# One kernel, a new order of its work: the turn of A alternates by head pair, early chunks take whole squares, and PSUM banks are named per product

## The chip, the cores and the metric

The kernel runs on one NeuronCore of a Trainium2 chip. A core has five engines that run side by side, each its own queue of instructions in order: TensorE (PE, matrix products; the loading of its weights is shown as PEld), VectorE (DVE), ScalarE (ACT), GpSimd (POOL) and SyncE (SP), which here only issues transfers. SBUF is the on-chip memory with 128 partitions, PSUM the accumulator memory with eight banks. Engines wait for each other by semaphores.

The metric is the device time of one execution in microseconds. It is compared between the kernel before and the changed one on the same chip.

## The reference

Linear attention with a decay for each head channel, then a feed-forward layer with an unusual activation on every token.

```python
# attention: 4 batches, 8 heads, 768 tokens, head size 48
state = 0
for t in range(768):
    cur = (u * k_t) outer v_t
    y_t = r_t @ (state + cur)
    state = w * state + k_t outer v_t        # w: 0.85 to 0.95 for each head and channel
x = y as [3072 tokens, 384]
# feed-forward, 384 -> 2048 -> 384
h = x @ w_in
g = h * erf(softplus(h))
out = g @ w_out
```

## The kernel before, in words

**Attention.** The 768 tokens are cut into 6 stretches of 128, times 4 batches: 24 chunks `g`, four of each stretch. The recurrence becomes products for each chunk. `K` and `R` scale k and r by powers of the decay (lines 187, 191), `V` (chunks 0 to 3) and `N` make the natural layout of k (201, 208, 195), `Qa`, `Qb`, `Qc` make the diagonal term q = sum of r·u·k (212, 215, 219). `M` lays q on the diagonal of a square for four heads at a time (230, 232). `A` multiplies k and r for each head into a square of 128 by 128 tokens in PSUM (249), `P` copies the half of it that is earlier in time over the `M` square, with a mask (255, copy_predicated). `Y` multiplies v with these squares and with the carried state (272), `D` is the chunk's contribution to the state (291) and `S` updates the state (303 to 309). `X` splits y into a rounded upper part and a rest, the input of the feed-forward layer (312, 315).

**The turn.** Heads come in four pairs; the head `hh` of a pair is 0 or 1. The second head of each pair has its tokens rolled by 64 in k, v and the natural layouts, so that the two heads of a pair fill opposite halves of the systolic array at the same time. `A` skips the quarter of each square that the mask would drop: one half of its products has 64 columns in place of 128, and `P` takes two instructions for a head set, one of 64 by 256 and one of 128 by 256.

**Feed-forward.** Tokens are taken 512 at a time, six blocks `b`, and the 2048 hidden channels 128 at a time: 96 steps of block by hidden slice, twice. Step `f` is nine products into one PSUM bank `h` (338), steps `a b z c d e g h l` make the activation on ACT and DVE (345 to 381; the last one, `l`, on DVE or POOL), and step `p` is nine products of the result into three accumulators (397). `O` moves accumulators out. The weights come as raw 64-bit words and are turned by steps `Ca` to `Cf` into two rounded parts (118 to 130); `F` fetches them.

**What sets the order.** All engines follow one long list of words, ORDER, written out by hand at line 614. Word by word, the kernel emits the step's instructions into the queues; a `+` puts the step on POOL, a `*` on ACT, and no mark on DVE. Within an engine nothing overtakes. `L` issues the two loads of a chunk (66, 69) into the queue of SP, which also runs in order, and a load waits there until its buffer is free: the chunks have three buffers and chunk 3 one of its own. `W` puts products of zeros on PE (87, dummy). PSUM: three banks `h` are handed out in turn to `f`, and before the feed-forward starts to some of the early products; `A0`, `A1` are for attention, `acc0` to `acc2` for the accumulators.

In the opening some 30 attention words and W words run on PE before the first `f` step, f0, which needs the x of chunks 0 to 3 and the first group of weights.

Of the kernel before, what the change touches and what calls it, by code (L numbers as in the profile page):

```python
# [26 lines left out]
P = 128  # L27
C = 128
D = 48
# [11 lines left out]
def body(ctx: ExitStack, tc: tile.TileContext, att, wcol, u, win, wout, levels, outT):  # L41
# [92 lines left out]
    ident = const.tile([P, 2, P], F32, name="ident")  # L134
    mask = const.tile([P, 2, P], F32, name="mask")
# [3 lines left out]
    for o, op, fill in ((ident, ALU.not_equal, 1.0), (mask, ALU.is_gt, 0.0)):  # L139
        for r, hh, j0 in ((slice(0, P), 0, 0), (slice(0, H), 1, H), (slice(H, P), 1, 0)):  # L140
            nc.gpsimd.affine_select(out=o[r, hh], in_=o[r, hh], pattern=[[1, P]], compare_op=op, fill=fill,
                                    base=-j0, channel_multiplier=-1)

# [20 lines left out]
    for r, h0 in ((slice(0, H), 0), (slice(H, PR), H)):  # L164
        nc.scalar.copy(out=wk[r, :, h0:h0 + H], in_=pw[r, 1])
        nc.vector.tensor_tensor(out=wk[r, :, H - h0:C - h0], in0=pw[r, 1],
                                in1=wp[r, 6, 1, :, None].to_broadcast([r.stop - r.start, NPAIR, H]), op=ALU.mult)
# [30 lines left out]
    def turn_k(g):  # L198
        tp = (ps3 if g < 4 else ps1).tile([P, NPAIR, PR], F32, tag="h" if g < 4 else "A1", name=f"kt{g}")
# [23 lines left out]
    def diag_m(q, g, hh, eng):  # L223
# [4 lines left out]
        if eng is nc.scalar:  # L228
            for p in range(NPAIR):
                nc.scalar.mul(out=m[:, p, :], in_=ident[:, hh], mul=q[:, p, hh:hh + 1])  # L230
        else:
            eng.tensor_tensor(out=m, in0=ident[:, hh:hh + 1].to_broadcast([P, NPAIR, C]),
                              in1=q[:, :, hh:hh + 1].to_broadcast([P, NPAIR, C]), op=ALU.mult)
        return m

    def a_step(g):

        t = chunks[g]
        if g in (0, 2):
            ap = [ps3.tile([P, NPAIR, C], F32, tag="h", name=f"A{g}_{hh}") for hh in range(2)]  # L240
        else:
            ap = [ps1.tile([P, NPAIR, C], F32, tag=f"A{hh}", name=f"A{g}_{hh}") for hh in range(2)]
# [10 lines left out]
    def predicated(am, ap, m, hh):  # L253
        for r, c in ((slice(H * hh, H * hh + H), slice(0, H)), (slice(0, P), slice(H, C))):
            nc.vector.copy_predicated(out=am[r, :, c], data=ap[r, :, c],  # L255
                                      mask=m[r, hh:hh + 1, c].to_broadcast([r.stop - r.start, NPAIR, H]))

    def y_step(g):
        s = st_[g]
        s["y"] = y_product(chunks[g], [s["am", 0], s["am", 1]], g % 4, g < 4, f"y{g}", f"acc{g % 2}" if g < 4 else "A0")  # L260

    def y_product(t, am, b, first, name, tag="A0"):
# [4 lines left out]
        y = ps1.tile([P, NQ, C], F32, tag=tag, name=name)  # L267
# [19 lines left out]
    def ds_product(t, first, name):  # L287
        ds = (ps3 if first else ps1).tile([PR, NPAIR, D], F32, tag="h" if first else "A1", name=name)
# [156 lines left out]
    for i, x in enumerate(words):  # L445
        eng = {"+": nc.gpsimd, "*": nc.scalar}.get(x[-1], nc.vector)
# [33 lines left out]
        elif what == "A":  # L480
            st_.setdefault(num, {})
            a_step(num)
        elif what == "P":
            predicated(st_[num // 10]["am", num % 10], st_[num // 10]["ap"][num % 10], mask.bitcast(U32), num % 10)
        elif what == "Y":
            y_step(num)
# [255 lines left out]
```

## Time and profile before

| | us |
|---|---|
| median of 3 runs | 528.97 (525.49 to 532.92) |
| span of the profiled execution | 527.4 |
| PE busy in it | 509.2 |
| ACT busy | 398.6 |
| DVE busy | 350.9 |
| POOL busy | 158.7 |

The span runs from the first to the last instruction. A busy PE is not PE at its peak: matmul records overlap, so 9 products whose records are 0.40 us each end 2.09 us apart as a group. The page cuts the span into 40 slices of 13.2 us. An idle time has a releaser behind it, the instruction whose end let the waiting one go.

### The profile page before, as it was taken

How to read it: one execution, taken by the hardware profiler on the slowest of the kernel's cores; microseconds unless marked ns; L12 is line 12 of the kernel's file. 1: busy time of each engine (PE TensorE's matmuls, PEld its weight loads, DVE VectorE, ACT ScalarE, POOL GpSimd, SP SyncE). 2: the span in 40 equal slices, each digit the busy share in tenths (PEclk: the TensorE clock that was granted, in tenths of full speed). 3: DMA queues.
4: the chain of work that ended last, by engine and by line, in shares of the span. 5: the costliest groups of instructions: out<-in, count | busy, mean ns of one | idle time of the engine just before them, and what ended most of it. 6: DMA issues, size and time to landing. Idle time of an engine off the chain costs nothing.

```text
span 527.4 us, 10451 instructions
## 1 busy us (share of the span) xinstructions
PE 509.2 (97%) x4164; PEld 393.0 (75%) x4164; DVE 350.9 (67%) x610; ACT 398.6 (76%) x765; POOL 158.7 (30%) x147
## 2 busy tenths in 40 slices
PE   7989999899999999999999999999999999999995
PEld 4547777678787778778787787787878777888883
DVE  6999998979787674869587643653664484343442
ACT  4587987889999784877766397767887676786883
POOL 5331225420222440353334434139600230100100
PEclk9999999999999999999999999999999999999999
DMA  8853373332421600531303322040030000010001
GB/s 299 315 195 122 121 251 132 112 128 87 155 99 40 236 21 1 188 155 41 137 1 98 139 88 87 2 162 15 35 115 0 2 1 1 16 45 2 0 1 66
DMA packets 13863, 48.91 MB, mean 93 GB/s; under 512 B 1648, under 2 KB 1776, under 8 KB 13808
## 3 DMA queue, kind: packets, MB, share of 16 engines
q1 hardware_dynamic: 13808, 48.18, 25.9%
q8 instruction: 35, 0.57, 0.4%
q14 instruction: 20, 0.16, 0.1%
HBM read 41.88 MB, written 6.29 MB: 91 GB/s over the span
## 4 chain that ended last, share of the span: by engine, by line
PE 79%; DVE 9%; DMA 4%; ACT 3%; POOL 2%; issue 2%; SPq 1%; POOLq 0%; ACTq 0%
PE h L338 34%; PE acc L397 33%; PE y L272 6%; DMA att<-in_att_dram 4%; PE A L249 3%; PE ds L291 1%; DVE s L370 1%; DVE am L255 1%; DVE wt L125 1%; DVE gl L381 1%; POOL gl L381 1%; PE dummy L87 1%; DVE s L354 1%; DVE wt L120 1%; DVE att L191 1%
## 5 line engine op out<-in xcount | busy, mean ns | idle before, releaser
L338 PE MATMUL h<-x,wih 128*128 128x512 f32 x576 | 183.0, 399 | 1.1 <-DVE s L370 1.1
L338 PEld LDWEIGHTS h<-x,wih 128*128 128x128 f32 x576 | 106.6, 188 | 28.5 <-DVE s L370 2.2
L397 PE MATMUL acc<-gh,woh 128*128 128x512 f32 x288 | 116.5, 404 | 1.4 <-ACT woh L128 1.4
L381 POOL TENSOR_TENSOR gl<-s,gh 128x512 fp32r<-128x512 f32 x43 | 56.7, 1321 | 201.0 <-ACT gh L376 200.9
L397 PE MATMUL acc<-gh,wol 128*128 128x512 f32 x288 | 114.0, 396 | 0.8 <-POOL wol L130 0.6
L397 PE MATMUL acc<-gl,woh 128*128 128x512 f32 x288 | 113.8, 395 | 0.2 <-DVE gl L381 0.2
L338 PE MATMUL h<-x,wil 128*128 128x512 f32 x288 | 113.8, 395 | 0.0
L370 DVE SCALAR_TENSOR_TENSOR s<-s,h 128x512 f32<-128x512 f32 x96 | 65.2, 683 | 63.2 <-ACT s L366 62.9
L354 DVE SCALAR_TENSOR_TENSOR s<-s,h 128x512 f32<-128x512 f32 x96 | 65.5, 684 | 53.1 <-ACT s L349 35.4
L376 ACT CAST gh<-s 128x512 fp32r<-128x512 f32 x96 | 59.1, 616 | 34.5 <-DVE s L370 20.7
L358 ACT ACTIVATE s<-s 128x512 f32<-128x512 f32 x96 | 60.2, 629 | 28.7 <-DVE s L354 28.3
L345 ACT ACTIVATE s<-h 128x512 f32<-128x512 f32 x96 | 56.5, 590 | 27.2 <-PE h L338 27.0
L397 PEld LDWEIGHTS acc<-gh,woh 128*128 128x128 f32 x288 | 54.2, 188 | 17.2 <-issue 2.6
L397 PEld LDWEIGHTS acc<-gh,wol 128*128 128x128 f32 x288 | 54.2, 188 | 14.2 <-POOL wol L130 1.0
L338 PEld LDWEIGHTS h<-x,wil 128*128 128x128 f32 x288 | 54.2, 188 | 12.8
L397 PEld LDWEIGHTS acc<-gl,woh 128*128 128x128 f32 x288 | 54.2, 188 | 12.6 <-DVE gl L381 0.8
L349 ACT ACTIVATE s<-s 128x512 f32<-128x512 f32 x96 | 60.0, 626 | 0.9
L362 ACT ACTIVATE s<-s 128x512 f32<-128x512 f32 x96 | 59.8, 627 | 1.0
L366 ACT ACTIVATE s<-s 128x512 f32<-128x512 f32 x96 | 59.7, 626 | 0.8
L381 DVE TENSOR_TENSOR gl<-s,gh 128x512 fp32r<-128x512 f32 x53 | 40.6, 768 | 19.1 <-ACT gh L376 18.8
L255 DVE COPY_PREDICATED am<-mask,A 64x256 f32<-64x256 uint32 x96 | 39.5, 442 | 11.9 <-ACT am L230 4.0
L230 ACT ACTIVATE am<-ident,q 128x128 f32<-128x128 f32 x100 | 30.8, 389 | 3.1 <-DVE q L219 3.0
(76 smaller groups left out, 498.2 us busy)
## 6 DMA issues: line engine op xcount, KB each, us to landing
att<-in_att_dram SPq DMA_DIRECT2D x24, 608.0 KB, 5.4
att<-in_att_dram SPq DMA_DIRECT2D x24, 512.0 KB, 4.0
raw<-in_win_dram SPq DMA_DIRECT2D x8, 768.0 KB, 4.3
raw<-in_wout_dram SPq DMA_DIRECT2D x8, 768.0 KB, 4.3
out_dram<-o SPq DMA_DIRECT2D x18, 256.0 KB, 2.2
part<-o SPq DMA_DIRECT2D x6, 256.0 KB, 2.1
o<-part SPq DMA_DIRECT2D x6, 256.0 KB, 3.8
ub<-in_u_dram SPq DMA_DIRECT2D x1, 192.0 KB, 2.5
```

What stands on the lines that cost most here:

```text
L255: nc.vector.copy_predicated(out=am[r, :, c], data=ap[r, :, c], mask=m[r, hh:hh + 1, c].to_broadcast([r.stop - r.start, NPAIR, H]))
L338: nc.tensor.matmul(out=h, lhsT=w[:, f, q, :], rhs=x[:, xi, q, :], start=k == 0, stop=k == 8)
L345: nc.scalar.activation(out=s1, in_=e["h"], func=AF.Tanh, bias=FB0, scale=FA0)
L349: nc.scalar.activation(out=s1, in_=s1, func=AF.Tanh, bias=FB1, scale=FA1)
L354: nc.vector.scalar_tensor_tensor(out=e["s"], in0=e["s1"], scalar=FG, in1=e["h"], op0=ALU.mult, op1=ALU.add)
L358: nc.scalar.activation(out=s, in_=s, func=AF.Tanh, bias=FB2, scale=FA2)
L362: nc.scalar.activation(out=s, in_=s, func=AF.Square, bias=FB3, scale=FA3)
L366: nc.scalar.activation(out=s, in_=s, func=AF.Square, bias=FB4, scale=FA4)
L370: nc.vector.scalar_tensor_tensor(out=s, in0=s, scalar=FC, in1=ff[n]["h"], op0=ALU.subtract, op1=ALU.mult, reverse0=True)
L376: nc.scalar.copy(out=e["gh"], in_=e["s"])
L381: eng.tensor_tensor(out=e["gl"], in0=e["s"], in1=e["gh"].bitcast(F32), op=ALU.subtract)
L397: nc.tensor.matmul(out=acc[e], lhsT=w[:, f, es], rhs=g, start=first and i == 0, stop=last and i == 2)
```

## The change

1. **The turn alternates by head pair.** The head that is rolled by 64 tokens is the second one in pairs 0 and 2 and the first one in pairs 1 and 3. `ident` and `mask` get a third square, so that pairs of squares can be read as (0, 1) or (1, 2). The set-up of wk takes four half-size copies and four half-size multiplications in place of two and two.
2. **Whole squares for chunks 0 to 7** (`FULL = 8`): all products of `A` have 128 columns, and `P` is one instruction of 128 by 512 for a head set. For chunks 8 to 23 `P` becomes three instructions: one of 128 by 256 and two of 64 by 128.
3. **Banks named per product**: a word may carry `@` and bank letters (`A0@hh`, `Y10@1`, `D11@0`), so that `A`, `Y` and `D` can lie in `A0`, `A1` or a bank of the ring `h`.
4. **ORDER is a new list** of as many words (1,723). Other words carry `+` and `*`: POOL has 12 more tensor_tensor instructions in all (145 for 133). The zeros of `W` are 62 products in both, 12 of them behind f0 (8 before).

```diff
-    for r, h0 in ((slice(0, H), 0), (slice(H, PR), H)):
-        nc.scalar.copy(out=wk[r, :, h0:h0 + H], in_=pw[r, 1])
+    for r, hh in ((slice(0, H), 0), (slice(H, PR), 1)):
+        for b in range(2):
+            h0 = H * ((hh + b) % 2)
+            nc.scalar.copy(out=wk[r, b::2, h0:h0 + H], in_=pw[r, 1, b::2])
...
-                    jc = abs(c0 - H * hh)
-                    nc.tensor.matmul(out=ap[hh][jc:jc + H, p, i0:C], lhsT=t[r, 512 + p * C + jc:512 + p * C + jc + H],
-                                     rhs=t[r, p * C + i0:(p + 1) * C], start=True, stop=True)
+                    jc = abs(c0 - H * ((hh + p) % 2))
+                    i = 0 if g < FULL else i0
+                    nc.tensor.matmul(out=ap[hh][jc:jc + H, p, i:C], lhsT=t[r, 512 + p * C + jc:512 + p * C + jc + H],
+                                     rhs=t[r, p * C + i:(p + 1) * C], start=True, stop=True)
...
+    def predicated(g, am, ap, m, hh):
+        if g < FULL:
+            nc.vector.copy_predicated(out=by_pair(am), data=by_pair(ap), mask=turned(m, hh))
+            return
+        for r, ps, t, c in ((slice(0, P), slice(0, NPAIR), None, slice(H, C)),
+                            (slice(0, H), slice(hh, NPAIR, 2), 0, slice(0, H)),
+                            (slice(H, P), slice(1 - hh, NPAIR, 2), 1, slice(0, H))):
...
+WARM, FULL = 16, 8
+BANKS = {"0": "A0", "1": "A1", "h": "h"}
...
-U0 L0a L0b L1a K0 T0 L1b R0 V0 Q0a A0 Q0b+ F00 R1+ Q0c N0* M00* W2 D0 S0b K1+ L2a S0a M01* P00 W5 A1 Q1a L2b P01 Q1b+
+U0 L0a L0b W2 K0 Q0a Q0b T0 L1a R1 V0 Q0c M01* L2a M00* L2b N0* R2 R0 L1b K2 F00 Q2a W5 W6 K1 Q1a Q1b+ A0@hh P00 P01
```

Line numbers move: 191, 215, 249, 255, 291, 315, 338, 397 of before are 201, 225, 259, 265, 310, 334, 357, 416 of the changed kernel.

The queue of DVE at the opening, from the first scaling of chunk 0 (its buffer is att_164 before and att_170 in the change; att_167 is chunk 1). Before:

```order
L187 TENSOR_TENSOR att_164<-att_164,wk 112x512
L191 TENSOR_TENSOR att_164<-att_164,wr 112x512
L212 TENSOR_TENSOR att_164<-att_164,ub 128x384
L219 TENSOR_REDUCE q_207<-att_164 128x8
L303 TENSOR_TENSOR sbd<-ds_219,wp 48x4x48 x2
L255 COPY_PREDICATED am_0_211<-mask,A_0_185 64x4x64
L255 COPY_PREDICATED am_0_211<-mask,A_0_185 128x4x64
L212 TENSOR_TENSOR att_167<-att_167,ub 128x384
L255 COPY_PREDICATED am_1_233<-mask,A_1_186 64x4x64
L255 COPY_PREDICATED am_1_233<-mask,A_1_186 128x4x64
```

and in the change (att_186 is chunk 1, att_201 chunk 2):

```order
L197 TENSOR_TENSOR att_170<-att_170,wk 112x512
L222 TENSOR_TENSOR att_170<-att_170,ub 128x384
L225 TENSOR_TENSOR att_170<-att_170 128x384
L201 TENSOR_TENSOR att_186<-att_186,wr 112x512
L229 TENSOR_REDUCE q_194<-att_170 128x8
L201 TENSOR_TENSOR att_201<-att_201,wr 112x512
L201 TENSOR_TENSOR att_170<-att_170,wr 112x512
L197 TENSOR_TENSOR att_201<-att_201,wk 112x512
L222 TENSOR_TENSOR att_201<-att_201,ub 128x384
L197 TENSOR_TENSOR att_186<-att_186,wk 112x512
L222 TENSOR_TENSOR att_186<-att_186,ub 128x384
L265 COPY_PREDICATED am_0_203<-mask,A_0_234 128x512
```

The second product for q0 (line 215, 225 in the change) moved from POOL to DVE, and scalings of chunks 1 and 2 stand where the queue went to the state and the masks of chunk 0.

The queue of SP just behind the loads of chunk 0, before:

```order
L66 DMA att_167<-in_att_dram 128x1024
L69 DMA att_167<-in_att_dram 128x1216
L102 DMA raw_204<-in_win_dram 128x768
L66 DMA att_230<-in_att_dram 128x1024
L69 DMA att_230<-in_att_dram 128x1216
L102 DMA raw_303<-in_wout_dram 128x768
L66 DMA att_328<-in_att_dram 128x1024
L69 DMA att_328<-in_att_dram 128x1216
L66 DMA att_384<-in_att_dram 128x1024
```

and in the change (att_337 is chunk 3, att_388 chunk 4):

```order
L66 DMA att_186<-in_att_dram 128x1024
L66 DMA att_201<-in_att_dram 128x1024
L69 DMA att_201<-in_att_dram 128x1216
L69 DMA att_186<-in_att_dram 128x1216
L102 DMA raw_215<-in_win_dram 128x768
L102 DMA raw_315<-in_wout_dram 128x768
L66 DMA att_337<-in_att_dram 128x1024
L66 DMA att_388<-in_att_dram 128x1024
L69 DMA att_337<-in_att_dram 128x1216
```

Chunk 2 moved ahead of the first weights, and the second half of chunk 3 behind the first half of chunk 4, which waits until a chunk's buffer is free.

On PE, the products D5 and D4 around the third `p` step (p2), before:

```order
L291 MATMUL ds_977<-att_454 48x48 x8
L397 MATMUL acc_0_916<-gh_951,woh 128x512
L397 MATMUL acc_0_916<-gl_956,woh 128x512
L397 MATMUL acc_0_916<-gh_951,wol 128x512
L397 MATMUL acc_1_917<-gh_951,woh 128x512
L397 MATMUL acc_1_917<-gl_956,woh 128x512
L397 MATMUL acc_1_917<-gh_951,wol 128x512
L397 MATMUL acc_2_918<-gh_951,woh 128x512
L397 MATMUL acc_2_918<-gl_956,woh 128x512
L397 MATMUL acc_2_918<-gh_951,wol 128x512
L291 MATMUL ds_1011<-att_384 48x48 x8
L338 MATMUL h_1024<-x_486,wih 128x512 x2
```

and in the change, between p1 and f5:

```order
L416 MATMUL acc_2_909<-gl_903,woh 128x512
L416 MATMUL acc_2_909<-gh_872,wol 128x512
L310 MATMUL ds_928<-att_388 48x48 x8
L310 MATMUL ds_937<-att_472 48x48 x8
L357 MATMUL h_953<-x_383,wih 128x512 x2
```

Two attention products that stood on either side of a feed-forward step stand together. Over the whole list PE goes from an attention product back to `f` or `p` 45 times behind f0 before, and 35 times in the change.

## Rows read from the trace of the kernel before

**Rows 1.** The page: the span, busy time of each engine, and DVE's busy share in 40 slices.

```profile
span 527.4 us, 10451 instructions
PE 509.2 (97%) x4164; PEld 393.0 (75%) x4164; DVE 350.9 (67%) x610; ACT 398.6 (76%) x765; POOL 158.7 (30%) x147
...
DVE  6999998979787674869587643653664484343442
```

**Rows 2.** Windows: busy time of PE, PEld, DVE, ACT and POOL in three stretches (start:end, length, then the engines with their instructions, the clock, DMA).

```profile
7.20:41.30 34.10, 29.86 (x479) 18.21 (x480) 31.74 (x63) 22.44 (x67) 13.93 (x12) 1.00 0.74 277
42.50:123.00 80.50, 76.90 (x682) 58.39 (x679) 73.43 (x116) 68.30 (x128) 25.68 (x21) 1.00 0.39 132
123.00:522.00 399.00, 396.41 (x2958) 313.44 (x2956) 240.06 (x405) 304.53 (x567) 115.27 (x100) 1.00 0.19 66
```

**Rows 3.** Timeline around f0: DVE's last x product of the opening, the end of Y4 on PE, and f0's first products.

```profile
40.77 0.54 DVE L315 TENSOR_TENSOR x<-y,x 128x384 fp32r<-128x384 f32 x1
...
41.52 1.06 PE L272 MATMUL y<-am,att 128*32 128x128 f32 x32
42.51 0.73 PE L338 MATMUL h<-x,wih 128*128 128x512 f32 x2
```

**Rows 4.** Waits of DVE between 7.2 and 41.3 us: total, times, longest.

```profile
DVE q L219 <- POOL att L215: 1.3, 2, 1.1
DVE sbd L303 <- PE ds L291: 0.7, 1, 0.7
```

**Rows 5.** Groups of DVE by form: count, busy us, mean ns, idle before.

```profile
L354 DVE SCALAR_TENSOR_TENSOR s<-s,h 128x512 f32<-128x512 f32 x96 | 65.5, 684 | 53.1 <-ACT s L349 35.4 <-POOL gl L381 16.5
...
L255 DVE COPY_PREDICATED am<-mask,A 64x256 f32<-64x256 uint32 x48 | 21.4, 445 | 11.6 <-ACT am L230 4.0 <-PE A L249 3.8 <-ACT gh L376 1.7
L255 DVE COPY_PREDICATED am<-mask,A 128x256 f32<-128x256 uint32 x48 | 21.1, 439 | 0.3
...
L130 DVE TENSOR_TENSOR wol<-wt,woh 128x768 fp32r<-128x768 f32 x6 | 5.7, 952 | 1.4 <-ACT woh L128 1.4
...
L303 DVE TENSOR_TENSOR sbd<-ds,wp 48x192 f32<-48x192 f32 x8 | 2.8, 353 | 0.7 <-PE ds L291 0.7
```

**Rows 6.** Timeline in the opening: POOL and DVE instructions on SBUF data that ran at the same time.

```profile
28.79 1.00 POOL L215 TENSOR_TENSOR att<-att 128x384 f32<-128x384 f32 x1
28.94 1.40 DVE L191 TENSOR_TENSOR att<-att,wr 112x512 f32<-112x512 f32 x1
...
48.86 0.68 DVE L191 TENSOR_TENSOR att<-att,wr 112x512 f32<-112x512 f32 x1
```

**Rows 7.** Timeline around 215 us: the same on a smaller tile, and it again a little later with POOL idle.

```profile
215.08 1.29 POOL L381 TENSOR_TENSOR gl<-s,gh 128x512 fp32r<-128x512 f32 x1 [20.91 <-ACT gh L376]
215.10 1.48 DVE L309 TENSOR_TENSOR sbd<-sbd,wp 48x192 f32<-48x192 f32 x1
217.46 0.34 DVE L309 TENSOR_TENSOR sbd<-sbd,wp 48x192 f32<-48x192 f32 x1
```

**Rows 8.** The chain that ended last, in order of time (start, us, what): feed-forward steps next to each other, and behind attention products.

```profile
164.87 4.21 PE acc L397 x18
169.07 1.67 PE y L272 x56
170.74 4.40 PE h L338 x18
175.14 0.49 PE ds L291 x16
175.63 2.30 PE h L338 x9
...
184.23 1.02 PE A L249 x24
185.25 4.39 PE acc L397 x18
```

**Rows 9.** Waits of PE, the longest from 42.5 to 123 us (first four) and from 123 us on (last two): total, times, longest.

```profile
PE acc L397 <- ACT woh L128: 1.4, 1, 1.4
PE ds L291 <- DVE am L255: 0.7, 1, 0.7
PE acc L397 <- POOL wol L130: 0.6, 1, 0.6
PE y L272 <- DVE am L255: 0.5, 2, 0.3
...
PE h L338 <- DVE s L370: 0.9, 1, 0.9
PE y L272 <- DVE am L255: 0.8, 1, 0.8
```

**Rows 10.** Timeline of the opening: a wait for a chunk's second half on POOL, and the first load that waits for a free buffer, on SP.

```profile
15.29 1.54 POOL L212 TENSOR_TENSOR att<-att,ub 128x384 f32<-128x384 f32 x1 [0.97 <-DMA att<-in_att_dram]
15.48 0.33 SPq L66 DMA_DIRECT2D att<-in_att_dram  x1
```

**Rows 11.** The end of the chain, the last copy of an accumulator, and PE's dummies before f0.

```profile
519.14 2.14 PE acc L397 x8
...
521.76 0.37 ACT L418 COPY o<-acc 128x256 f32<-128x256 f32 x1 [0.32 <-DVE o L417]
...
39.89 1.02 PE L87 MATMUL dummy<-warm 128*128 128x512 bf16 x4 [0.78 <-PE A L249]
```

More of the change, by code (lines that the diff above doesn't have):

```diff
@@ L198, in turn_k @@
     def turn_k(g):
-        tp = (ps3 if g < 4 else ps1).tile([P, NPAIR, PR], F32, tag="h" if g < 4 else "A1", name=f"kt{g}")
+        tp = bank("h" if g < 4 else "A1", [P, NPAIR, PR], f"kt{g}")
         for p in range(NPAIR):
@@ L229, in diag_m, with bank, a_step @@
             for p in range(NPAIR):
-                nc.scalar.mul(out=m[:, p, :], in_=ident[:, hh], mul=q[:, p, hh:hh + 1])
+                nc.scalar.mul(out=m[:, p, :], in_=ident[:, (hh + p) % 2], mul=q[:, p, hh:hh + 1])
         else:
-            eng.tensor_tensor(out=m, in0=ident[:, hh:hh + 1].to_broadcast([P, NPAIR, C]),
-                              in1=q[:, :, hh:hh + 1].to_broadcast([P, NPAIR, C]), op=ALU.mult)
-        return m
-    def a_step(g):
+            eng.tensor_tensor(out=by_pair(m), in0=turned(ident, hh),
+                              in1=by_pair(q[:, :, hh:hh + 1]).to_broadcast([P, NPAIR // 2, 2, C]), op=ALU.mult)
+        return m
+    def bank(tag, shape, name):
+        return (ps3 if tag == "h" else ps1).tile(shape, F32, tag=tag, name=name)
+    def a_step(g, tags):
         t = chunks[g]
[L239 to L242, printed above, removed]
+        ap = [bank(tags[hh], [P, NPAIR, C], f"A{g}_{hh}") for hh in range(2)]
         for p in range(NPAIR):
@@ L285, in y_product, with ds_product @@
         return y
-    def ds_product(t, first, name):
-        ds = (ps3 if first else ps1).tile([PR, NPAIR, D], F32, tag="h" if first else "A1", name=name)
+    def ds_product(t, tag, name):
+        ds = bank(tag, [PR, NPAIR, D], name)
         for h in range(8):
@@ L445, in body @@
     for i, x in enumerate(words):
+        x, _, where = x.partition("@")
         eng = {"+": nc.gpsimd, "*": nc.scalar}.get(x[-1], nc.vector)
@@ L481, in body @@
             st_.setdefault(num, {})
-            a_step(num)
+            a_step(num, [BANKS[c] for c in where or "01"])
         elif what == "P":
-            predicated(st_[num // 10]["am", num % 10], st_[num // 10]["ap"][num % 10], mask.bitcast(U32), num % 10)
+            predicated(num // 10, st_[num // 10]["am", num % 10], st_[num // 10]["ap"][num % 10], mask.bitcast(U32), num % 10)
         elif what == "Y":
-            y_step(num)
+            y_step(num, BANKS[where] if where else f"acc{num % 2}" if num < 4 else "A0")
         elif what == "X":
@@ L489, in body @@
         elif what == "D":
-            st_.setdefault(num, {})["ds"] = ds_product(chunks[num], num < 4, f"ds{num}")
+            st_.setdefault(num, {})["ds"] = ds_product(chunks[num], BANKS[where] if where else "h" if num < 4 else "A1", f"ds{num}")
         elif what == "S":
@@ new lines @@
+g45 h45 l45 Q17a+ Q17b+ Q17c S12c+ R17+ a47 b47 h46 S11d+ Y15 X15a X15b z47 Y16@1 X16a M171+ M170 A17@0h P170 c47 d47
+D15@h p45 l46 e47 X16b g47 h47 N16+ S15a l47 S13d L18a K18 P171 p46 p47 Y17@1 R18 L18b Q18a+ O311c O471a S15b O470a
+O470b X17a N17 Q18b N18 A18@0h f48 a48 f49 Q18c O471b M181 P181 b48 O472a f50 z48 c48 a49 b49 d48 M180+ P180 X17b e48
+a50 b50 g48 S14d+ Y18 z49 D18 c49 d49 S18a h48 S18b f51 l48 D16 p48 e49 S15c z50 a51 c50 g49 h49 l49+ X18a X18b b51
+z51 d50 e50 f52 L19a K19+ c51 S18c d51 g50 p49 f53 h50 S16a e51 g51 h51 l50+ p50 a52 l51 b52 p51 z52 a53 b53 S16b z53
@@ L702, in turn @@
         x = x.copy()
-        if rows:
-            x.reshape(B * nc_, P, NPAIR, C)[:, 64:] = np.roll(x.reshape(B * nc_, P, NPAIR, C)[:, 64:], C // 2, axis=3)
-        else:
-            x.reshape(B * nc_, C, H, Dh)[:, :, 1::2] = np.roll(x.reshape(B * nc_, C, H, Dh)[:, :, 1::2], C // 2, axis=1)
+        for h in range(H):
+            if (h // 2 + h) % 2:
+                if rows:
+                    s = x.reshape(B * nc_, 2, P // 2, NPAIR, C)[:, h % 2, :, h // 2]
+                    s[:] = np.roll(s, C // 2, axis=2)
+                else:
+                    s = x.reshape(B * nc_, C, H, Dh)[:, :, h]
+                    s[:] = np.roll(s, C // 2, axis=1)
         return x
```

170 lines of the change are left out of this document (87 added, 83 removed).

## Prediction

> **What bounds the kernel now.** I read the page first: PE is busy for 509 of 527.4 us, and DVE's slices are full at the start and fall to a half at the end [rows 1]. Then three windows [rows 2]. From 7.2 to 41.3 us, the opening, DVE works 31.7 of 34.1 us while PE fills its time with dummies. From 42.5 to 123 us PE is idle for 3.6 us of 80.5, with DVE at 73.4 and ACT at 68.3 us close behind it. From 123 to 522 us PE is idle for 2.6 us of 399, and 0.7 us of that lies behind its last product, which ends at 521.3 [rows 11]; DVE has 159 us free there. So there are two stages with different limits: before f0 the queue of DVE, behind f0 the sum of PE's work. f0 itself started at 42.5, when Y4 ended on PE; its last x product had ended 1.2 us sooner, at 41.3 [rows 3]. Last the waits: in the opening DVE waits 1.3 us for POOL and 0.7 for PE [rows 4]; behind f0 PE's waits are single ones of 0.3 to 1.4 us, for weights, masks and an `h` bank [rows 9]. Behind f0 nothing that PE computes goes away, so the change can give: an earlier f0, fewer waits, fewer crossings between attention and feed-forward.
>
> **The sum is made against the profiled span of 527.4 us.** The median of the three runs is 528.97, 1.6 us above it; I add 1.6 at the end.
>
> **1. The opening, f0 earlier by 4.1 us.** Between chunk 0's first scaling and the last x that f0 needs, the two lists give DVE the same 9 scalings of 512 columns, 6 products of 384, 6 reductions and 4 x products. Different are three things. *Masks*: 11 head sets as 22 half instructions, now 10 as whole ones. A half takes 0.44 us alone [rows 5], and follows the one ahead after about 0.40, so 8.8 us. No row shows a mask copy of 512 columns. Its floor is one half, 0.44, its ceiling two, 0.80; I take 0.65, from the nearest row, 512 columns read from PSUM in 0.68 [rows 5], so 6.5 us: 2.3 less (bounds 0.8 and 4.4). *Weights*: the last step of the first w_out group went to POOL: 0.95 less. *State*: one `S` of 0.35 more. DVE's work falls by 2.9 us. Its own waits were 2.4 us of this stretch [rows 2, 4]. The reduction of q0 followed a product on POOL, which is now on DVE, and scalings of chunks 1 and 2 stand where DVE waited for D0. They need their loads, and chunk 2 now comes ahead of the first weights; before, POOL waited 0.97 us for chunk 2's second half, which came at 15.3 behind them [rows 10]. I take half of the idle time back, 1.0 us (bounds 0 and 2.0). The 1.2 us between last x and f0 go too: in the new list four DVE words, about 2 us, stand between the last mask of chunk 4 and the last x, so Y4's 1.67 us run beside them. Against this stand 0.2 us for the set-up of wk (two more small instructions on DVE and on ACT), and 0.8 us for one more meeting of DVE and POOL on SBUF: the row of one such meeting is 1.40 us in place of 0.68 [rows 6]. The third squares of `ident` and `mask` lie on POOL before it has chunk work: nothing. Sum: 2.9 + 1.0 + 1.2 - 0.2 - 0.8 = 4.1 us, f0 at 38.4.
>
> **2. Whole squares on PE: nothing.** `A` for one chunk takes 1.02 us with half its products at 64 columns [rows 8]: 32 records, 32 ns each. `Y` has 56 records, all of 128 columns, in 1.67 us, 30 ns each. So columns up to 128 seem to be free where products of small tiles follow each other. If they are not, `A` costs 256/192 of 1.02, 0.34 us more; of the eight chunks only 6 and 7 lie behind f0, so 0.7 us is the upper bound. The Trainium skill, "TensorEngine Tiling (Array Packing)", section Instruction Overhead, says that a matmul has some 60 cycles of overhead, and that one column takes as long as sixty. By that the 64-column products are just past the overhead, and the whole squares would cost the 0.7 us; the rows of Y speak for nothing, and no run here has shown either.
>
> **3. Fewer crossings: 1.9 us less.** A feed-forward step behind another takes 2.10 us; behind `Y`, `D` or `A` it takes 2.29 or, as a pair, 4.40 in place of 4.21 [rows 8]. That is 0.19 us for each return, 45 before and 35 in the change: 1.9 us. The pair D4, D5 shows one. This rests on PE having no wait there, or else the time goes into the wait (bound 0).
>
> **4. Dummies: 0.85 us more.** Four more zeros stand behind f0, four in 1.02 us with overlap [rows 11], 0.21 each. They cost nothing if PE would wait there.
>
> **5. Waits from f0 to the twelfth `p`: 1.8 us less.** The 3.6 us [rows 2] come from weights and masks that DVE and POOL finish late [rows 9]. By the counts of the two lists DVE has about 5 us less to do between f0 and p12 (masks of chunks 5 to 9, products moved to POOL), PE 1 us less, ACT 3 us less. I take half (bounds: 0, 3.6).
>
> **6. Waits behind that: 1.1 us more.** For chunks 8 to 23 each mask is three instructions. 0.44 for the one of 256 columns, and for 64 by 128 between 0.23 and 0.35 (48 by 192 took 0.35 [rows 5]): 0 to 0.26 us more for each of 32, up to 8 us, beside DVE's 159 free us; uncovered it is 0.26 ahead of a `Y`. What worries more: in the new list several multiplications of the state on POOL, 0.95 us each, stand right ahead of the `Y` that reads the state (S6c and Y10, S11d and Y15, S14d and Y18, S15d and Y19); before, 20 us of PE work lay between. One late word costs up to 1 us, and PE already pays 1.9 us of waits there. I take 1.1 us more, four such places at a quarter of a us (bounds -1.9 and +4). The end of the list keeps its shape: f95, five `p` steps, then 6.1 us of copies and transfer.
>
> **Sum:** 527.4 - 4.1 - 1.9 + 0.85 - 1.8 + 1.1 = 521.55, with 1.6 us: **523.2 us**, 1.1% less.
>
> **Rivals.**
> *All of it fits (chance 0.17).* f0 at 37.5, that is 5.0 us, with every load in time and no meeting with POOL; all 5.5 us of PE's waits gone; crossings 1.9, dummies paid. 527.4 - 5.0 - 5.5 - 1.9 + 0.85 = 515.9, or 517.5 as a run. For it speaks that DVE, the bound of the opening and close to PE behind it, loses work in both. Against it: waits of a list this tight do not all vanish.
> *POOL holds DVE up (chance 0.18), slower than before.* A state product took 1.48 us beside a POOL product that began 0.02 us ahead of it, and 0.34 with POOL idle [rows 7]; the scaling in the opening took 1.40 beside POOL's 1.00 [rows 6]. 12 more POOL instructions, many in the opening and in the stretch to p12 where DVE is the bound, at 0.7 to 1.1 us each, cost DVE 8 to 13 us. Taking 10.5 us with all of it passed on to PE: 521.55 - 0.8 (in term 1 already) + 10.5 = 531.2, 532.8 as a run. It decides the sign from 6.7 us lost on the path, the 5.9 saved and that 0.8. Against it: most meetings fall where DVE has time to spare.
> The Trainium skill, "SBUF — State Buffer", section Who interferes with whom, says that a DVE instruction with two SBUF inputs and a POOL instruction that reads SBUF exclude each other for the whole instruction, whichever comes first. By that rule the forecast's 0.8 us would be too small if more than one of the moved products meets a scaling; the rows agree with the rule (1.48 beside 0.34).
> *The time is given back (chance 0.15).* f0 starts 4 us earlier and then PE waits for DVE, since work that stood ahead of f0's x now stands behind it: both masks of chunk 5 (one before) and the three steps of the second w_in group come on DVE between f0 and f2. Or the second half of chunk 3, now queued on SP behind a load that waits for Y0's buffer (such a load went out at 15.5 us before [rows 10]), comes after its product is due on DVE and holds up everything behind it. Terms 1 and 5 go, terms 3, 4 and 6 stay: 527.4 - 1.9 + 0.85 + 1.1 = 527.5, 529 as a run.
>
> **How the numbers follow.** The forecast, 523.2, has a chance of 0.50 and by its bounds runs from 519 to 527. The rivals have 0.17, 0.18 and 0.15. For eight in ten, I leave out the lower half of the first rival and the upper half of the second, and reach from 517 to 530.5. 2% of 528.97 is 10.6 us, about what a measurement of this kernel can tell from no change. Faster by over 2% means under 518.4: most of the first rival, 0.14. Slower by over 2% means over 539.5: the far end of the second, with POOL in the way twice as often, 0.04. Within 2%: 0.82.
>
> **What would show it.** In the changed profile f0's first product should start near 38.4 us; the mask copy of 128 by 512 should take about 0.68 us; DVE's waits up to f0 should be under 1.5 us; `A` of an early chunk should last 1.02 us on PE; PE's idle time from f0 to p12 should be about 2 us. If f0 starts at 41 or later, the opening was misjudged: long DVE rows beside POOL speak for the second rival, a DVE wait on chunk 3's load for the third. If f0 is early and PE's idle time behind it grew by as much, it is the third. The prediction is wrong if PE has waits of several us at the Y steps named in term 6.

## The result, and the profile after

The changed kernel takes 513.92 us (median of 4 runs, 512.71 to 515.19) where the kernel before takes 530.19 on the same chip: ratio 0.971 (95% interval 0.965 to 0.977), 2.9% faster. I had forecast 523.2 with 517 to 530.5, and given "faster by over 2%" a chance of 0.14. The profiled execution went from 527.4 to 513.3 us. The page of after (answers to [rows 1]):

```profile
span 513.3 us, 10468 instructions
PE 501.4 (98%) x4164; PEld 391.9 (76%) x4164; DVE 348.7 (68%) x624; ACT 400.4 (78%) x735; POOL 180.5 (35%) x161
...
DVE  7999999899786675666687768567555644333443
```

Of the 14.1 us, 7.8 are less PE work (509.2 to 501.4) and 6.3 less time in which PE doesn't work. Of the 7.8, 6.0 lie behind f0, where the forecast had 1.05 (1.9 for crossings less 0.85 for zeros). Windows of after (columns as in [rows 2]: opening, the 80 us behind f0, the rest):

```profile
7.20:36.60 29.40, 28.24 (x479) 17.55 (x481) 27.79 (x53) 19.38 (x60) 17.44 (x12) 1.00 0.81 297
37.60:118.10 80.50, 78.78 (x684) 61.28 (x681) 75.34 (x115) 73.53 (x131) 33.08 (x23) 1.00 0.45 152
118.10:507.70 389.60, 388.55 (x2959) 310.27 (x2957) 240.32 (x431) 304.03 (x539) 124.84 (x110) 1.00 0.19 65
```

PE's idle time in the three stretches was 4.2, 3.6 and 2.6 us and is 1.2, 1.7 and 1.1. The clock is 1.00 in all of them, so it plays no part between before and after. Timeline around f0 in after (answers to [rows 3]):

```profile
36.07 1.47 DVE L334 TENSOR_TENSOR x<-y,x 128x384 fp32r<-128x384 f32 x3
...
36.62 1.06 PE L291 MATMUL y<-am,att 128*32 128x128 f32 x32
...
37.60 0.73 PE L357 MATMUL h<-x,wih 128*128 128x512 f32 x2
```

f0 starts at 37.60, not 42.51: 4.9 us of the 14.1. The chain of after, in order of time (start, us, what; answers to [rows 8]):

```profile
60.74 0.85 PE ds L310 x32
...
274.01 3.20 PE y L291 x112
...
407.38 0.81 PE A L259 x24
408.19 4.40 PE acc L416 x18
412.59 0.81 PE A L259 x24
413.40 2.31 PE acc L416 x9
415.71 2.10 PE h L357 x9
```

The reader is to see the 0.81: a late `A` took 1.02 us in [rows 8]. For 16 chunks that is 3.4 us, and no term of the forecast has it. A return to the large products still costs about 0.2 us (2.31 beside 2.10). Two `Y` next to each other take 3.20, not 2 x 1.67, and two `D` 0.85, not 2 x 0.49. PE's waits of after (total, times, longest; answers to [rows 9]):

```profile
PE dummy L87 <- ACT warm L81: 2.4, 1, 2.4
PE A L259 <- issue: 1.6, 1, 1.6
PE A L259 <- POOL att L201: 0.5, 1, 0.5
PE h L357 <- DVE s L389: 0.5, 1, 0.5
PE y L291 <- DVE am L265: 0.5, 1, 0.5
```

The first stands at the very start, before and after alike. The waits for weights are gone, and at the `Y` steps that term 6 feared none came. The 1.6 us at `A` is nearly all that PE still waits from f0 to p12, and it is a new wait. The view names no releaser; the timeline shows DVE's scaling for this `A` (chunk 7) beside a POOL product that began 0.05 us sooner:

```profile
72.02 1.27 POOL L197 TENSOR_TENSOR att<-att,wk 112x512 f32<-112x512 f32 x1 [4.40 <-DMA att<-in_att_dram]
72.07 1.77 DVE L201 TENSOR_TENSOR att<-att,wr 112x512 f32<-112x512 f32 x1
...
73.94 1.10 PE L259 MATMUL A<-att 48*64 48x128 f32 x32 [1.61 <-issue]
```

Alone this scaling takes 0.68 us, so 1.1 of the 1.6 are the meeting. The masks, by form (count, busy us, mean ns):

```profile
L274 DVE COPY_PREDICATED am<-mask,A 64x128 f32<-64x128 uint32 x64 | 18.9, 296 | 0.5
L271 DVE COPY_PREDICATED am<-mask,A 128x256 f32<-128x256 uint32 x32 | 14.3, 448 | 4.8 <-PE A L259 2.4 <-POOL am L242 1.9
...
L265 DVE COPY_PREDICATED am<-mask,A 128x512 f32<-128x512 uint32 x16 | 11.3, 731 | 0.0
```

A whole square costs 0.73 us (I took 0.65), a late mask in three instructions 0.448 + 2 x 0.296 = 1.04.

### The profile page after: what moved, and what is told of

It is laid out like the page before. It is cut to its first block, busy times and chain, and to the rows that moved or that the text cites. A ratio compares the mean times of both kernels' runs of the same rounds, so it can differ in the third digit from the quotient of the medians.

```text
span 513.3 us, 10468 instructions
## 1 busy us (share of the span) xinstructions
PE 501.4 (98%) x4164; PEld 391.9 (76%) x4164; DVE 348.7 (68%) x624; ACT 400.4 (78%) x735; POOL 180.5 (35%) x161
## 4 chain that ended last, share of the span: by engine, by line
PE 82%; DMA 9%; DVE 3%; issue 2%; POOL 1%; ACT 1%; SPq 0%; POOLq 0%; ACTq 0%
PE acc L416 37%; PE h L357 35%; DMA att<-in_att_dram 6%; PE y L291 6%; PE A L259 3%; DMA raw<-in_win_dram 2%; PE ds L310 1%; DMA out_dram<-o 1%; DVE wt L125 1%; POOL gl L400 1%; DVE am L265 0%; ACT wt L118 0%; DVE sbd L322 0%; DVE att L201 0%; POOL am L242 0%
## 5 line engine op out<-in xcount | busy, mean ns | idle before, releaser
L400 POOL TENSOR_TENSOR gl<-s,gh 128x512 fp32r<-128x512 f32 x45 | 59.7, 1327 | 186.1 <-ACT gh L395 159.7
L400 DVE TENSOR_TENSOR gl<-s,gh 128x512 fp32r<-128x512 f32 x51 | 37.5, 734 | 19.2 <-ACT gh L395 19.0
L242 POOL TENSOR_TENSOR am<-ident,q 128x512 f32<-128x512 f32 x20 | 24.2, 1214 | 43.2 <-DVE q L229 40.9
L259 PEld LDWEIGHTS A<-att 48*64 48x64 f32 x768 | 18.9, 133 | 10.5 <-issue 6.9
```

Of the source, the lines that this page charges most:

```text
L259: nc.tensor.matmul(out=ap[hh][jc:jc + H, p, i:C], lhsT=t[r, 512 + p * C + jc:512 + p * C + jc + H], rhs=t[r, p * C + i:(p + 1) * C], start ...
L400: eng.tensor_tensor(out=e["gl"], in0=e["s"], in1=e["gh"].bitcast(F32), op=ALU.subtract)
```

## The experiments

Theory after the result: three separate gains, an earlier f0 and a quieter stretch behind it by the new order, and a cheaper `A` by the alternating turn. Rival: the order alone does it all, and the turn only comes along. In the table, ratios are to the kernel before on the same chip; f0 and the late `A` are from each profile. The kernel before had medians of 528.3 to 530.2 us beside these runs, so medians of two rows compare to a us or two, and neighbouring intervals overlap in places. In the openings of four profiles PE's granted clock fell to 0.5, the lower of its two levels, for a stretch (turn_full from 35.0 us, after_full0 from 41.3, after_swapback from 30.3, old_open from 19.1), each time soon after PE had stood idle for 1.7 to 2.4 us (idle times of 2.6 us in turn_only and 2.8 in swap_before were not followed by a fall); their f0 holds some of that.

| kernel | median us | ratio (95%) | f0 | late A |
|---|---|---|---|---|
| before, profiled | 528.97 | 1 | 42.51 | 1.02 |
| turn_only | 532.82 | 1.009 (1.006 to 1.012) | 47.54 | 0.81 |
| turn_full | 529.01 | 1.002 (1.000 to 1.005) | 45.57 | 0.81 |
| swap_before | 529.25 | 1.000 (0.996 to 1.004) | 44.85 | 1.02 |
| order_only | 518.52 | 0.981 (0.978 to 0.984) | 39.01 | 1.02 |
| order_full | 517.67 | 0.978 (0.973 to 0.983) | 38.26 | 1.02 |
| after_full0 | 522.86 | 0.989 (0.984 to 0.993) | 44.42 | 0.81 |
| **after** | 513.92 | 0.971 (0.965 to 0.977) | 37.60 | 0.81 |
| after_even_whole | 516.83 | 0.977 (0.972 to 0.982) | 37.66 | 1.03 |
| after_swapback | 513.82 | 0.970 (0.966 to 0.975) | 40.84 | 0.81 |
| after_group | 522.74 | 0.989 (0.985 to 0.993) | 40.27 | 1.21 |
| new_open | 524.25 | 0.993 (0.990 to 0.995) | 38.88 | 0.81 |
| old_open | 519.10 | 0.982 (0.976 to 0.987) | 45.33 | 0.81 |
| uncross | 522.11 | 0.987 (0.983 to 0.992) | 36.92 | 0.81 |

### The turn and the order, one at a time

**turn_only**: the changed code with the old list, no whole squares.

```diff
-WARM, FULL = 16, 8
+WARM, FULL = 16, 0
...
-U0 L0a L0b W2 K0 Q0a Q0b T0 L1a R1 V0 Q0c
+U0 L0a L0b L1a K0 T0 L1b R0 V0 Q0a A0@hh
```

> The old order of words with the turn that alternates by head pair, and no whole square: every mask copy is three instructions. Theory (alternating the turn shortens A on TensorE, because the second half of one pair and the first half of the next then use the same two corners of the array): A lasts 0.83 us in place of 1.02 in all 24 chunks, 18 of them behind f0, 3.4 us less; the third mask instruction costs VectorE 0.15 us each, some 1.5 us ahead of f0 and as much again up to 123 us; in sum 1 to 3 us less, ratio about 0.996. Rival (A is shorter in the changed kernel because of where the new order puts it): A stays at 1.02 us and the time rises by 1 to 3 us.

**turn_full**: the same with `FULL = 8`, that is the changed kernel with only the list put back.

> The old order of words with the alternating turn and whole squares for chunks 0 to 7. Theory: A of chunks 8 to 23 lasts 0.83 us, of 0 to 7 about 1.03; the masks of the first chunks cost 0.73 in place of 0.85 us a head set, so f0 comes about 1.3 us earlier; 3.0 us less for A and 1 to 2 for the opening, ratio about 0.991. Rival (the turn and the squares do nothing by themselves, all of the gain is the order): ratio 0.998 to 1.002, f0 within 0.5 us of 42.5.

**order_only**: the new list and banks, the old turn, masks in two instructions, no whole squares.

```diff
-                    jc = abs(c0 - H * ((hh + p) % 2))
+                    jc = abs(c0 - H * hh)
...
-WARM, FULL = 16, 8
+WARM, FULL = 16, 0
```

> The new order of words and the banks named per product, with the old turn and no whole square (two mask instructions for each head set in all chunks). Theory: A stays at 1.02 us, f0 comes 1 to 1.5 us later than in the changed kernel, at about 39; waits and returns behind f0 as in the changed kernel; about 9 us less than before, ratio 0.983. Rival (the new order pays only together with shorter A and P, since it is planned for them): waits behind f0 grow to 5 us or more and the ratio is above 0.99.

Measured: with the old list the cheaper `A` is there, 0.81 us from the first late chunk to the last, but f0 is 5.0 us later with three-instruction masks and 3.1 later with whole squares, and the time is 0.9% and 0.2% above before, where I had expected 0.4% and 0.9% below. From f0 to the start of the last product both are faster than before (477.0 and 475.9 us, before 478.4): what the turn saves behind f0 is lost ahead of it. The order alone brings 1.9%. So the order is about two thirds of the gain, and turn with whole squares bring the rest only in the new order (513.9 beside 518.5), not in the old one.

**order_full** and **after_full0** complete the square: whole squares without the alternating turn, and the turn without whole squares (`FULL = 0`), both in the new order.

```diff
# order_full
-                    jc = abs(c0 - H * ((hh + p) % 2))
+                    jc = abs(c0 - H * hh)
# after_full0
-WARM, FULL = 16, 8
+WARM, FULL = 16, 0
```

> The new order with the turn of the kernel before (not alternating) and whole squares for the first eight chunks; masks of the late chunks are two instructions. It differs from the new order alone by the whole squares only, and from the changed kernel by the turn only. Theory (turn and whole squares are two gains that add up: 16 x 0.21 = 3.4 us of A behind f0 from the turn, about 1.4 us of an earlier f0 from the whole squares): A of the late chunks 1.02, of the early ones about 1.03, f0 at 37.6 to 38.5, time about 517. Rival (the whole squares bring nothing unless the turn alternates): f0 at 39.0, time 518.5 as with the order alone; or, if the turn's A is what the time hangs on less than thought, 514 to 515.

> The changed kernel without whole squares: every chunk's second products have half the columns, and every mask is made of three instructions. Theory (the whole squares are a matter of VectorE in the opening): A of the first eight chunks falls from about 1.03 to 0.81 us of TensorE, but each half of a mask goes from 0.73 to about 1.04 us of VectorE; some eleven of them lie before f0, 11 x 0.31 = 3.4 us, so that f0 stands at 39.5 to 41; behind f0 three chunks give back 0.7: time about 516.5. Rival (TensorE, not VectorE, sets f0): 512 to 513.5, for 8 x 0.22 = 1.8 us less of A.

Measured: whole squares alone bring f0 0.75 us forward (39.01 to 38.26); the intervals of the two times overlap. The turn alone loses: f0 at 44.42, 6.8 us later than in after, though I expected 2 to 3.5. Ten head sets ahead of f0 in three instructions are 10 x 0.31 = 3.1 us of DVE, and about 2.0 come from meetings, below. Another 1.5 are PE's own: it waited 2.35 us for a mask, and then Y4 ran at half the clock, from 41.27 to f0 at 44.42, 3.15 us in place of 1.67:

```profile
41.27 1.51 PE L291 MATMUL y<-att,sbd 112*32 112x128 f32 x24 [2.35 <-DVE am L274]
42.51 1.98 PE L291 MATMUL y<-am,att 128*32 128x128 f32 x32
```

So the whole squares are what makes the turn affordable for DVE in the opening.

### What makes A cheap

A product of `A` uses one corner of the array, 48 of its 64 rows and all of its 64 columns; the products of the two heads of a pair lie on opposite corners, one diagonal, and run together.

**swap_before**: the kernel before with the two halves of `A` exchanged in the odd head pairs, so that the corners of the array in use change half as often.

```diff
-            for c0, i0 in ((0, 0), (H, H)):
+            for c0, i0 in ((0, 0), (H, H))[::1 - 2 * (p % 2)]:
```

> The kernel before, in which only the order of the two halves of A is turned round for pairs 1 and 3 (128 and 64 columns, 64 and 128, and so on). The turn of the heads is as before, and all other engines do the same. Theory (a change of corners of the array costs, not the turn as such): A lasts 0.83 us and the time falls by 0.19 x 18 = 3.4 us, ratio 0.9936. Rival (it is the alternating turn itself): A stays at 1.02 us, ratio 1.000.

**after_swapback**: the same edit in the changed kernel.

> The changed kernel with the two halves of A's products exchanged for the odd head pairs: the turn, the masks and the order of words stay, only the sequence of products on the array differs. The corners of the array now change at every step again, as in the kernel before (whole on one diagonal, half on the other, half on the first, whole on the second). Theory (changes of corners, or a half followed by a whole on the same corners, make A cheaper; the alternating turn itself does nothing): the late A goes back from 0.81 to about 1.02 us, 16 x 0.21 = 3.4 us, and the time is about 517.3. Rival (it is the turn, or the places in the accumulators that it writes, which makes A cheap, whatever the sequence): A stays at 0.81 us and the time at 514.

**after_group**: the changed kernel with all products on one diagonal of the array first, then all on the other.

```diff
-        for p in range(NPAIR):
-            for c0, i0 in ((0, 0), (H, H)):
+        for d in range(2):
+            for p in range(NPAIR):
+                c0 = i0 = H * ((d + p) % 2)
```

> The changed kernel, with A's products sorted by the pair of array corners that they use: first the eight products of every head pair that lie on the two corners of one diagonal, then the eight of the other. So the corners change once in an A, not three times as in the changed kernel (in the kernel before seven times); lengths still alternate, whole and half columns. Nothing else differs. Theory (what an A loses is a price for each change of corners between neighbouring products, (1.02 - 0.81) / 4 = 0.05 us each): A of the late chunks goes from 0.81 to about 0.71 us, the 16 of them give back 1.6 us, and the time is about 512. Rival (what counts is that on the same corners a short product is followed by a long one, and not the number of changes, as the kernel before with swapped halves suggests, whose A stayed at 1.02 with four changes fewer): here on each diagonal long and short alternate throughout, so A stays at 0.81 or falls a little, and the time is that of the changed kernel, 513 to 515.

**after_even_whole**: late chunks take the second product whole in pairs 0 and 2.

```diff
-                    i = 0 if g < FULL else i0
+                    i = 0 if g < FULL or p % 2 == 0 else i0
```

> The changed kernel in which the second product of each head, of half the columns, is taken with all its columns for the head pairs 0 and 2 of the late chunks too (those of pairs 1 and 3 stay halves). One diagonal of the array then carries four whole steps an A, the other two whole and two half ones. What A's products took so far: 1.02 us where one diagonal had four whole and the other four half steps, 0.81 where each had two and two, whatever the sequence, and 1.03 with eight whole steps. Theory (the fuller diagonal sets the time of an A, and what the other carries meanwhile is free): the late A goes from 0.81 to about 1.02 us, 16 x 0.21 = 3.4 us more, time about 517.3. Rival (the sum of the columns sets it, on a line between 0.81 for twelve and 1.03 for sixteen units): half of the halves filled, about 0.92 us, 1.8 us more, time about 515.6. The mean of the late A in the trace decides.

A late `A` in the chain, first after_even_whole:

```profile
319.10 1.03 PE A L259 x27
```

then after_group:

```profile
324.04 1.21 PE A L260 x28
```

and after_swapback:

```profile
319.53 0.81 PE A L259 x24
```

The number of changes of corners explains nothing: four in place of seven left 1.02 at 1.02 (swap_before), seven in place of four left 0.81 at 0.81 (after_swapback), and a single change made it worst, 1.21 (the changed kernel has four, not the three of that expectation). My theory of a price per change fell, and so did its rival that a half must be followed by a whole on the same corners. What agrees with all: each head pair makes two steps, one of whole and one of half products, each on one diagonal (two corners). In the kernel before one diagonal got every whole step and the other every half step. With the alternating turn each gets two of both. If the fuller diagonal sets the time of an `A` and the other works beside it, four whole steps are 1.02 us and two whole with two half steps 0.81; eight whole steps, four on each, should again take 1.02, and the early `A` of after_swapback takes 1.03. after_even_whole was made to tell this from a price of the columns: it fills one diagonal with four whole steps and leaves the other at two and two. The fuller diagonal gives 1.02, a sum of columns 0.92; it took 1.03. The single records of the traces say the same: each product stands there as two, and on one diagonal the next record starts some 0.109 us behind a whole one and 0.056 us behind a half one. Eight whole records are 0.87 us, four whole and four half ones 0.66, each with 0.15 more at the ends 1.02 and 0.81. after_group shows the condition: the diagonals must come in turn. One after the other they cover each other only in a small part (twice 0.66 is 1.32), and `A` goes to 1.21 and, of an early chunk, to 1.52.

The Trainium skill, "TensorEngine Tiling (Array Packing)", section Key Properties, says that different tiles of the array can load weights and multiply in parallel. The runs agree where neighbouring products lie on different corners (0.81 beside 1.21).

### The opening, the rest, and the returns

**new_open**: the new list's words ahead of f0, then what is left of the old list in its old sequence (ten of those words stood ahead of f0 there and still do). **old_open**: the reverse. Both with the changed code.

```diff
# new_open
-X2b X3a X3b X1b f0 M50* P50 L6b C01a C01b C01c M51* C01d P51 a0 f1 X4a C01e
+P50 W4 C01a K6 f0 X4a C01b C01c X4b C01d f1 a0 b0 Q6b F11 C01e Q6c N6+
# old_open
-X2b X3a X3b X1b f0 M50* P50 L6b C01a C01b C01c M51* C01d P51 a0 f1 X4a C01e
+X3b C01a K6 S3a f0 C01b C01c C01d P51 a0 f1 X4a C01e b0 Q6b X4b a1 z0
```

> The changed code with the new order's words up to the first input product f0, and behind them the words of the old order in their old sequence. So the opening is the changed one, and the rest is the old rest with the new code. Theory (the order's gain is made in two places: f0 some 4.9 us earlier, and behind f0 fewer waits and ten returns less, 2.7 + 1.9 us): f0 stands at 37.6 to 39, the old rest keeps its waits of 4 to 6 us behind f0, and the alternating turn gives its 3.4: time about 518 to 520. Rival A (the gain lies in the opening alone): about 514 to 516. Rival B (the rest loses again what the opening gains, since the old rest is tuned to a later f0): 524 to 529.

> The changed code with the old order's words up to f0, and behind them the words of the new order in their new sequence: the counterpart of the kernel with the new opening and the old rest. Theory (the rest's gain is its own, made of fewer returns to large products and of no waits, and doesn't need an early f0; the old opening loses to meetings of VectorE with GpSimd): f0 at 44.5 to 46 as with the old order and the new code, and from f0 to the end 475 to 477 us as in the changed kernel: time about 521 to 523. Rival (the opening is most of it): 525 to 528. Second rival (a late f0 is caught up behind it): 514 to 517.

Measured: new_open has the early f0, 38.88, but from there to the start of the last product it takes 477.3 us (after 469.8), and the time is 524.3, not the 518 to 520 of my theory but where rival B had it. Its PE is busy for 505.8 us, 4.4 more than after, and its waits for weights and masks are back. old_open has the late f0, 45.33, but then only 466.5 us: 3.3 of the lost 7.7 are caught up, and the time is 519.1, better than I expected. Of the 3.3, 2.0 are fewer waits of PE (A7 waits 0.5 us there, not 1.6, since its scaling met no POOL product) and 1.3 less PE time: four zeros of `W` fewer stand behind f0, and from Y5 to the next `f` it takes 2.36 us (49.72 to 52.08), not 3.44 (42.00 to 45.44). Rival B's reason, a rest that doesn't fit the early f0, isn't needed: from turn_full, which is the changed code with the whole old list, new_open gains 4.8 us, old_open 9.9 and after, with both, 15.1. So the rest of the order is worth more than the opening, about 10 us beside 5, and an early f0 is passed on only in part.

**uncross**: the changed list with 13 attention products moved apart, so that PE returns from a small to a large product 45 times behind f0, not 34 (the expectation has 44; counted in the list there are eleven more).

```diff
-p1 D4 D5@0 F12 C11e C11f+ a4 b4 f5 h2
+p1 D4 F12 C11e C11f+ a4 b4 f5 D5@0 h2
...
-b3 D6 S6a f4 X6a
+b3 f4 D6 S6a X6a
```

> The changed kernel with its order altered in 13 places only: where two products of the attention (Y, A, D) stand next to each other on TensorE, an input or output product of the feed-forward is put between them. So TensorE goes back from a small product to the large ones 44 times behind f0, and not 34 times, as it did 45 times in the kernel before. Theory (the price of a return that the prediction took, 0.19 us each): 10 x 0.19 = 1.9 us more, time about 515.8. Rival (a return costs nothing by itself, the 0.19 us being only where the model of the ends puts the last product): 513 to 514.5. A third way: a moved product waits for what used to be ready, which shows as a wait with a name on TensorE.

The page of uncross, and its PE waits:

```profile
PE 505.1 (97%) x4164; PEld 391.2 (75%) x4164; DVE 348.9 (67%) x624; ACT 400.7 (77%) x735; POOL 180.0 (35%) x161
```

```profile
PE h L357 <- DVE s L389: 1.4, 2, 0.9
PE acc L416 <- DVE gl L400: 1.1, 1, 1.1
PE A L259 <- PE h L357: 0.8, 1, 0.8
PE A L259 <- DVE att L201: 0.6, 2, 0.4
PE h L357 <- DVE x L334: 0.6, 1, 0.6
PE h L357 <- ACT x L331: 0.6, 1, 0.6
```

It is 8.2 us slower than after by the medians and 6.9 by the profiled executions, where I expected 1.9. PE is busy for 3.7 us more, and waits with names come on top, the third way of the expectation. The 3.7 are about eleven returns of 0.19 and as many neighbourhoods undone at 0.14 (two `Y` alone 3.34, together 3.20): 2.1 + 1.5. I had counted the way back and not the way in. And 13 words out of place brought 2 to 3 us of waits, which shows how tight the new order is.

### Meetings of DVE and POOL

The opening of one list can differ by 2 us between kernels that give DVE and POOL the same instructions: f0 stands at 42.51 in before and at 44.85 in swap_before. One such place, timeline of before:

```profile
22.35 0.69 DVE L191 TENSOR_TENSOR att<-att,wr 112x512 f32<-112x512 f32 x1
...
22.78 1.38 POOL L187 TENSOR_TENSOR att<-att,wk 112x512 f32<-112x512 f32 x1 [4.54 <-DMA att<-in_att_dram]
```

and of swap_before, where the load let POOL go 0.56 us sooner:

```profile
22.22 1.33 POOL L187 TENSOR_TENSOR att<-att,wk 112x512 f32<-112x512 f32 x1 [3.99 <-DMA att<-in_att_dram]
22.34 1.76 DVE L191 TENSOR_TENSOR att<-att,wr 112x512 f32<-112x512 f32 x1
```

Whoever begins first keeps its pace, and the other pays: 1.76 us beside 0.69 for DVE. In the changed kernel DVE begins first:

```profile
20.55 0.69 DVE L201 TENSOR_TENSOR att<-att,wr 112x512 f32<-112x512 f32 x1 [0.81 <-DMA att<-in_att_dram]
20.66 3.67 POOL L197 TENSOR_TENSOR att<-att,wk 112x512 f32<-112x512 f32 x2 [1.04 <-DMA att<-in_att_dram]
```

and in after_full0, shifted by its longer masks, POOL:

```profile
20.87 2.94 POOL L197 TENSOR_TENSOR att<-att,wk 112x512 f32<-112x512 f32 x2
...
21.28 1.41 DVE L201 TENSOR_TENSOR att<-att,wr 112x512 f32<-112x512 f32 x1
```

turn_full has five such losses of DVE ahead of f0 (four of 0.8 us, one of 1.1: 4.3), before two (1.5). The 2.8 between them is the largest part of its later f0, but not the only one: its masks give 1.6 us back, DVE waits 3.6 us from 7 us on in place of 2.0, and PE ran at half the clock for a stretch. The loss shows in the scalings, which read two operands from SBUF, and in line 120 of the weights; masks and reductions keep their length. The Trainium skill, "SBUF — State Buffer", section Who interferes with whom, gives this rule (the one that issues first blocks the other for the whole instruction), and the rows agree: 1.76 is 0.69 and most of the 1.21 that POOL still had to go. No run changed a meeting alone, so the share of f0 that they carry is read from rows, not tested by itself.

## Why the prediction was wrong

The stages were read rightly: DVE bounds the opening, PE's own work the rest. Steps in the order of the sum:

- **Term 1, the opening: 4.1 forecast, 4.9 measured.** Right in kind. Masks came out at 0.73 us alone and 0.68 in a row, near the 0.65. The one more meeting, 0.8 against, was wrong in sign: DVE's five scalings with wr (line 201) took 0.684 us each, and 0.986 before. That is 1.5 us gained, as the group of DVE up to 38 us shows, first before:

```profile
L191 DVE TENSOR_TENSOR att<-att,wr 112x512 f32<-112x512 f32 x5 | 4.9, 986 | 0.1
```

  and after:

```profile
L201 DVE TENSOR_TENSOR att<-att,wr 112x512 f32<-112x512 f32 x5 | 3.3, 684 | 0.8 <-DMA att<-in_att_dram 0.8
```

  On the other side, that the third squares on POOL cost nothing was wrong. The powers of the decay stand behind them in POOL's queue, and DVE waits for them; a wait of DVE in after:

```profile
DVE pw L166 <- POOL pw L157: 1.0, 1, 1.0
```

  The same wait was 0.2 before, in every kernel with three squares 0.7 to 1.0.
- **Term 2, whole squares on PE: nothing.** Its number held against the kernel before: an early `A` takes 1.03 to 1.10 us. Its reason did not: columns are not free. With the same turn a whole early `A` takes 1.03 us and one with halves 0.83 (A7 of after and of after_full0, start to next start); against before the filled halves cost nothing because they lay on the emptier diagonal, so the number was luck. The step that failed, the largest miss of the sum, is beside it: I listed the turn as a matter of masks and set-up and never asked what it does to the products themselves. It makes each late `A` 0.21 us shorter, 3.4 in all. order_full and after, and after_even_whole and after, show it from two sides: 3.8 and 2.9 us of the median, though the intervals of their ratios overlap a little, so that the size rests on the rows of `A`. The bound of this term should have reached below nothing.
- **Term 3, crossings: 1.9.** The mechanism was right and the size too small: uncross puts 3.7 us of PE work on eleven returns and as many ways in.
- **Term 4, the zeros: 0.85.** No run moved them alone; the place in old_open that has four fewer takes 1.1 us less, near the 0.85. PE's work in the two windows behind f0 fell from 473.3 to 467.3 us: 3.4 for `A`, and 2.6 for crossings less zeros, which is 3.7 less 1.1.
- **Term 5, waits to p12: 1.8.** 3.6 went to 1.7: the number is right, in part by luck. The old waits are gone altogether, where I took half, and 1.6 us came new at A7, 1.1 of them from a meeting of DVE and POOL that the term didn't have.
- **Term 6, later waits: +1.1.** Wrong in sign: 2.6 us of idle time, of which 0.7 lie behind the last product, went to 1.1, so 1.9 us of waits to 1.1. The products that I feared, POOL's state multiplications right ahead of `Y`, appear in no wait of PE. I had priced them at 0.95 us each from two long rows; of the 17 in the profile before 14 took 0.50 to 0.51. Which words of the new order bring this was not taken apart further.

The sum of what was measured: 4.9 for f0, 3.4 for `A`, 2.6 for crossings less zeros, 3.4 of idle time behind f0, less 0.2 behind the last window: 14.1. The forecast's 521.55 is 8.2 us above the 513.3. Of these, 3.4 are the turn, which had no price; 2.5 terms 5 and 6 (3.2 gained with the end, 0.7 forecast); 1.5 crossings and zeros (2.6 for 1.05); 0.8 f0. The rival *All of it fits* came nearest, 517.5, and it failed at the same place: without the price of the turn it could not go below 515.9. *POOL holds DVE up* did not occur in the opening, where the meetings went the other way, though turn_full shows it there; behind f0 it occurred once on PE's path, 1.1 us at A7. *The time is given back* did not occur either; its load is seen in one execution, the profiled one of after_swapback (with 516.55 us the slowest of its four), where chunk 3's second half came 2.4 us late for DVE:

```profile
26.38 0.56 DVE L222 TENSOR_TENSOR att<-att,ub 128x384 f32<-128x384 f32 x1 [2.44 <-DMA att<-in_att_dram]
```

There f0 stands at 40.84, with PE at half the clock from 30.3 us on as a second reason, and the median of that kernel is still that of after.

What stays open: which words of the new list take the old waits away. The 1.6 us at A7 are still in the changed kernel, and no run moved that meeting. No experiment here beat the changed kernel; after_swapback equals it.

## What to carry to other kernels

Where small products share the array, count the work of each set of corners and not the products: an edit that only moves work to the emptier corners shortened the step here (1.02 to 0.81 us), and work added there was free (1.02 to 1.03), as long as the corners came in turn. An instruction that is moved in a list also changes who begins first where two engines meet, and a tenth of a microsecond there decides over one; so read meetings from the trace of the very list, and give a new list a wide range. An edit can save in one stage and cost as much in another (the turn with whole squares in the old order: 2.5 us less behind f0, 3.1 more ahead of it), so read its worth stage by stage and not from the total.

## What was not expected of the hardware

- `A` with the same columns in all took 0.81, 1.02 or 1.21 us by where and in which order its products lie on the array.
- The same DVE scaling takes 0.69 or 1.76 us beside the same POOL product, by which of the two began first, 0.12 us apart.
- Small products next to each other save on both sides: a `Y` behind a `Y` 0.14 us, beside the 0.19 of the return.
